# Start-up and last store of a fused attention and mixer kernel: first head's scores with decay by one-hot matmuls, a new order of the first pairs, moved fillers, last output in two parts

## The chip, the cores and the metric

The kernel runs on one core of one Trainium2 chip. The metric is the time of one execution on the device in microseconds.

## The reference

Attention with a causal mask and a learned decay (8 batches, 8 heads, 576 positions, head size 64), then a mixer: a low-rank mix along the sequence and a two-layer ReLU mix along the channels. Cut to what matters here:

```python
scores = (q @ k.T) / sqrt(D)
cum    = cumsum(maximum(s, 0))              # s: (batch, head, position)
scores = where(causal, -1e9, scores + minimum(-(cum[i] - cum[j]), 0))
x      = softmax(scores) @ v                # (B, S, H*D)
u      = x + (x.T @ U @ V).T                # low rank, along the sequence
out    = u + relu(u @ w_ch1) @ w_ch2        # 512 -> 2048 -> 512
```

The decay adds `cum[j] - cum[i]` to every score. The kernel folds it into the score matmul: beside the 64 rows of q and k it appends four rows, so that the contraction over 68 rows gives the product and the decay together.

## The kernel before

Heads come in pairs (`n`), 32 in all, four to a batch. The start handles the four pairs of batch 0 by hand; afterwards a loop weaves attention and mixer so that TensorE stays full. Only the start and the end are touched by the change. `...` marks cuts.

The rows of the decay for all 64 heads are made at once, one head to a partition, with the cumulative sum split in three bf16 parts so that no precision is lost. The first four pairs get them by DMA from SBUF to the `slot` tiles, where the score matmul reads them below the 64 rows of q and k:

```python
nc.vector.tensor_tensor_scan(cum, s_sb, s_sb, 0.0, op0=ALU.add, op1=ALU.max)
nc.scalar.mul(rows[:, 3, 0, :], cum, -1.0)
nc.vector.tensor_copy(rows[:, 0, 1, :], cum)          # three parts: rows 0, 1, 2
...
for n in range(PB):
    for hh in range(2):
        nc.sync.dma_start(out=slots[n][D:KA, hh, 0 : 2 * S], in_=rows[2 * n + hh : ...])
```

Scores of a pair are four groups, each followed by one exp on ScalarE: the near scores of either head (1,024 columns each), a wide group for both heads (1,024 columns) and a small one (128 columns). `pscore` tiles rotate through two buffers, `pwork` tiles through four.

```python
def scores(n, pT):
    for hh in range(2):
        near = pscore()
        ...                                            # six matmuls, slot[0:68]
        nc.scalar.activation(pT[:, hh, 0:1024], near, EXP, scale=scale)
        yield
    mid, tail = pscore(), pwork()
    ...                                                # wide group, exp; small group, exp
```

`spin` issues matmuls on constant data whose results nobody reads. The text calls them fillers. The start of batch 0, in program order, where `T` transposes a pair, `S` makes its scores, and `v_tiles` brings the raw values into the layout that the last attention matmul wants:

```python
spin_some(9); step(T0); spin_some(2); step(T0, T0); spin_some(8)
step(T1); spin_some(4); step(T1, T1); spin_some(2); step(T2, T2, T2); spin_some(2)
step(S0); spin_some(1, pwork); step(S0); spin_some(1, pwork); step(S0, S0)
masks(pT_of(0), False)                                 # on VectorE
spin_some(2, pwork); step(S1); spin_some(2, pwork); step(T3, T3, T3); step(S1)
spin_some(2, pwork); step(S1, S1); spin_some(2, pwork)
masks(pT_of(1), True); load_w1(1)                      # masks on GpSimd
step(S2, S2); spin_some(2, pwork); v_tiles(0, (0, 1), ...); step(S2, S2)
...
v_tiles(0, (2, 3), ...); step(S3); v_tiles(0, (4,), ...); step(S3)
drain(values(0, pT_of(0))); step(S3, S3)
```

The end writes 128 rows of 512 columns at a time: 16 matmuls, an add on VectorE, a store of 256 KB.

The softmax here doesn't subtract the row's maximum and nothing guards it: scores larger than these inputs give would overflow.

## Time and profile before

| | before |
|---|---|
| time, median of 3 (lowest to highest) | 385.93 us (385.05 to 386.65) |
| span of the profiled execution | 383.5 us |
| TensorE busy | 373.1 us, 97% |
| second layer and first layer of the channel mix | 138.9 + 134.9 us |
| first exp of scores | 12.85 us |
| last wide exp of the first batch | 25.71 us |

The page of the kernel before: busy time of each engine, then, in 40 equal slices of the span, the busy tenths of TensorE and the clock that was granted to it, then the two costliest groups (busy us and mean ns of one, then idle time just before them).

```profile
PE 373.1 (97%) x3562; PEld 210.2 (55%) x3562; DVE 224.6 (59%) x464; ACT 193.7 (51%) x291; POOL 64.7 (17%) x100
...
PE   8899999999999999999999999999999999999996
...
PEclk9999999999999999999999999999999999999999
...
L595 PE MATMUL pwork<-w_sb,hT 128*128 128x512 bf16 x576 | 138.9, 379 | 0.4 <-DVE slot L311 0.3
L585 PE MATMUL pwork<-uT,w_sb 128*128 128x512 bf16 x560 | 134.9, 379 | 0.6 <-DVE x_sb L400 0.3
```

TensorE shows 90% or more everywhere but in the first two slices and the last. The two large groups are 71% of the span and have almost no idle time before them, so nothing but the start and the end can give time without fewer matmuls.

The chain of waits of the kernel before, around the first exp (start us, us, what):

```profile
7.45 0.76 ACT slot L311
8.21 3.93 DMA slot<-hT
12.15 0.05 issue
12.19 0.63 PE pscore L334 x6
12.82 0.02 issue
12.85 1.03 ACT pT L348
```

The first scores wait 3.93 us for four rows of 2.3 KB. In that time ScalarE makes two copies (1.61 us, from 9.76) and is otherwise idle: 1.50 us before them and 1.48 us after them, until the first exp.

ScalarE's timeline of the kernel before, from there to the last exp of the batch (start us, us, what, count, and in brackets idle time before it with its releaser):

```profile
12.85 1.94 ACT L348 ACTIVATE pT<-pscore 128x1024 bf16<-128x1024 f32 x2 [1.48 <-PE pscore L334]
14.67 1.03 ACT L356 ACTIVATE pT<-pscore 128x1024 bf16<-128x1024 f32 x1
15.57 0.30 ACT L362 ACTIVATE pT<-pwork 128x128 bf16<-128x128 f32 x1
15.73 2.18 ACT L348 ACTIVATE pT<-pscore 128x1024 bf16<-128x1024 f32 x2
...
18.87 1.96 ACT L348 ACTIVATE hT<-pscore 128x1024 bf16<-128x1024 f32 x2
21.46 1.02 ACT L356 ACTIVATE hT<-pscore 128x1024 bf16<-128x1024 f32 x1 [0.63 <-PE pscore L334]
22.38 0.27 ACT L362 ACTIVATE hT<-pwork 128x128 bf16<-128x128 f32 x1
23.27 2.11 ACT L348 ACTIVATE hT<-pscore 128x1024 bf16<-128x1024 f32 x2 [0.61 <-PE pscore L334]
25.71 1.02 ACT L356 ACTIVATE hT<-pscore 128x1024 bf16<-128x1024 f32 x1 [0.34 <-PE pscore L334]
```

Read it as a relay. Up to 18.87 the exps follow each other, so ScalarE is the limit. From 21.46 on each begins after an idle time that TensorE ends: now TensorE's order is the limit, since it puts value selection and fillers between the score groups. The mixer cannot begin until the last exp here and the values after it are done.

The end, in the timeline of the kernel before:

```profile
376.35 0.69 DVE L632 TENSOR_TENSOR o_sb<-pwork,u_sd 128x512 f32<-128x512 f32 x1 [2.76 <-PE pwork L595]
377.07 3.79 SPq L649 DMA_DIRECT2D out_dram<-o_sb  x2
379.80 0.69 DVE L632 TENSOR_TENSOR o_sb<-pwork,u_sd 128x512 f32<-128x512 f32 x1 [2.76 <-PE pwork L595]
```

After the last matmul come the last add (0.69 us) and a store; its last landing in the trace is at 382.52, 2.72 us after that add began.

### The profile page before, as it was taken

The numbers are of one execution on the slowest core, as the hardware profiler recorded it, in microseconds if no ns is written. First come the engines' busy times: TensorE is split into PE (matmuls) and PEld (weight loads), VectorE is DVE, ScalarE is ACT, GpSimd is POOL, SyncE is SP. The second block draws the span as 40 slices with busy tenths as digits, with TensorE's granted clock in tenths as the row PEclk, the third lists the DMA queues.
The fourth block names the chain that finished last, engine by engine and source line by source line (L and its number), as shares of the span: only waits on it lengthen the run. The fifth ranks groups of instructions, "written<-read, shape, count | busy, mean of one in ns | idle before, by whom it ended". The sixth has DMA issues, their size and how long they took to land.

```text
span 383.5 us, 8466 instructions
## 1 busy us (share of the span) xinstructions
PE 373.1 (97%) x3562; PEld 210.2 (55%) x3562; DVE 224.6 (59%) x464; ACT 193.7 (51%) x291; POOL 64.7 (17%) x100
## 2 busy tenths in 40 slices
PE   8899999999999999999999999999999999999996
PEld 3565455665665666555655665666555544444442
DVE  8873556978778776777668766786663132002011
ACT  3865985356743576237733674357552520621610
POOL 8976316005100600060006000000000000000000
PEclk9999999999999999999999999999999999999999
DMA  7999999927992995299249933320323031302002
GB/s 113 161 210 186 195 174 106 166 63 110 147 56 72 163 150 42 70 172 152 34 53 161 173 41 49 95 77 20 62 59 99 19 81 58 82 28 83 0 29 82
DMA packets 85966, 37.29 MB, mean 97 GB/s; under 512 B 66408, under 2 KB 80200, under 8 KB 85928
## 3 DMA queue, kind: packets, MB, share of 16 engines
q0 software_dynamic: 47216, 18.44, 48.8%
q1 hardware_dynamic: 38712, 18.31, 24.9%
q8 instruction: 28, 0.46, 0.5%
q14 instruction: 10, 0.08, 0.1%
HBM read 37.25 MB, written 9.70 MB: 122 GB/s over the span
## 4 chain that ended last, share of the span: by engine, by line
PE 85%; DVE 7%; ACT 4%; DMA 2%; issue 1%; DVEq 0%; ACTq 0%; POOLq 0%
PE pwork L595 30%; PE pwork L585 30%; PE pscore L334 10%; PE pwork L390 6%; PE pwork L294 3%; DVE slot L311 3%; ACT pT L348 1%; DVE x_sb L400 1%; ACT slot L311 1%; DMA slot<-hT 1%; DMA q_sd<-in_q_dram 1%; PE pscore L585 1%; DVE uT L444 1%; PE pwork L516 1%; PE pwork L419 1%
## 5 line engine op out<-in xcount | busy, mean ns | idle before, releaser
L595 PE MATMUL pwork<-w_sb,hT 128*128 128x512 bf16 x576 | 138.9, 379 | 0.4 <-DVE slot L311 0.3
L585 PE MATMUL pwork<-uT,w_sb 128*128 128x512 bf16 x560 | 134.9, 379 | 0.6 <-DVE x_sb L400 0.3
L617 ACT ACTIVATE hT<-pwork 128x512 bf16<-128x512 f32 x140 | 84.4, 608 | 83.9 <-PE pwork L585 83.6
L311 DVE COPY slot<-pwork 64x576 bf16<-64x576 bf16 x118 | 94.4, 800 | 11.5 <-PE pwork L294 9.7
L348 ACT ACTIVATE pT<-pscore 128x1024 bf16<-128x1024 f32 x58 | 58.4, 1025 | 67.1 <-PE pscore L334 66.9
L595 PEld LDWEIGHTS <-hT 128*128 128x128 bf16 x576 | 50.6, 98 | 52.0 <-issue 2.2
L585 PEld LDWEIGHTS <-w_sb 128*128 128x128 bf16 x576 | 51.0, 98 | 51.0 <-issue 1.2
L632 DVE TENSOR_TENSOR o_sb<-pwork,u_sd 128x512 f32<-128x512 f32 x32 | 22.1, 690 | 67.5 <-PE pwork L595 66.5
L334 PE MATMUL pscore<-slot 68*128 68x128 bf16 (+4 forms) x512 | 55.9, 245 | 2.1 <-ACT slot L311 0.8
L334 PEld LDWEIGHTS <-slot 68*128 68x128 bf16 x576 | 42.4, 97 | 26.1 <-issue 2.3
L321 DVE TENSOR_TENSOR pT<-pT,keep 128x512 bf16<-128x512 bf16 (+1 forms) x84 | 29.5, 353 | 37.5 <-ACT pT L362 23.3
L390 PEld LDWEIGHTS <-pT 128*128 128x128 bf16 x870 | 32.4, 98 | 10.0 <-issue 0.3
L390 PE MATMUL pwork<-v_slot,pT 128*128 128x65 bf16 x870 | 34.6, 193 | 0.0
L356 ACT ACTIVATE pT<-pscore 128x1024 bf16<-128x1024 f32 x29 | 30.1, 1039 | 4.7 <-PE pscore L334 3.2
L400 DVE TENSOR_TENSOR x_sb<-pwork,rec 128x320 bf16<-128x320 f32 x64 | 31.3, 491 | 2.1
L108 POOL DMA_DIRECT2D q_sd<-in_q_dram x12 | 9.4, 782 | 126.8 <-PE pwork L294 117.1
L226 POOL DMA_DIRECT2D v_slot<-in_v_dram x24 | 21.4, 906 | 9.4 <-DMA w_sb<-in_moe_w_ch_dram 8.8
L294 PEld LDWEIGHTS <-q_sd 72*128 72x128 bf16 x256 | 15.1, 99 | 11.2 <-DMA q_sd<-in_q_dram 1.0
L399 DVE RECIPROCAL rec<-pwork 128x5 f32<-128x5 f32 x64 | 12.0, 190 | 15.4 <-PE pwork L390 14.8
L294 PE MATMUL pwork<-identity,q_sd 72*128 72x72 bf16 x256 | 18.2, 197 | 0.2
L294 PE MATMUL pwork<-identity,k_sd 72*128 72x72 bf16 x256 | 17.9, 197 | 0.3 <-DMA k_sd<-in_k_dram 0.3
L294 PEld LDWEIGHTS <-k_sd 72*128 72x128 bf16 x256 | 12.3, 98 | 0.9 <-DMA k_sd<-in_k_dram 0.4
(101 smaller groups left out, 191.8 us busy)
## 6 DMA issues: line engine op xcount, KB each, us to landing
out_dram<-o_sb SPq DMA_DIRECT2D x36, 256.0 KB
w_sb<-in_moe_w_ch_dram POOLq DMA_DIRECT2D x4, 1024.0 KB, 12.2
q_sd<-in_q_dram POOLq DMA_DIRECT2D x6, 576.0 KB, 8.9
k_sd<-in_k_dram POOLq DMA_DIRECT2D x6, 576.0 KB, 14.6
v_slot<-in_v_dram POOLq DMA_DIRECT2D x24, 128.0 KB, 15.8
hT<-in_v_dram POOLq DMA_DIRECT2D x2, 512.0 KB, 12.4
q_sd<-in_q_dram POOLq DMA_DIRECT2D x4, 144.0 KB, 4.5
k_sd<-in_k_dram POOLq DMA_DIRECT2D x4, 144.0 KB, 5.1
```

What stands on the lines that cost most here:

```text
L294: nc.tensor.transpose(tps[hh][:, c, t2, :], src[:, 2 * hp + hh, ds(t2 * 128, 128)], identity[:TP, :TP],)
L311: copies(n, hh, par)(dst[:, :, :, :, par], tp[par * D : par * D + D].rearrange("p c t m -> p c m t"),)
L321: nc.vector.tensor_tensor(dst, dst, keep[:, :, 0:w].to_broadcast([128, n_tiles, w]), op=ALU.min)
L334: nc.tensor.matmul(dst, lhsT=slot[0:KA, hh, ds(S + j * 128, 128)], rhs=slot[0:KA, hh, lo:hi], start=True, stop=True,)
L348: nc.scalar.activation(pT[:, hh, 0:1024], near, EXP, scale=scale)
L356: nc.scalar.activation(pT[:, :, 1024:1536], mid.rearrange("p (a b) -> p a b", a=2), EXP, scale=scale)
L390: nc.tensor.matmul(po[:, i, :], lhsT=pT[:, hh, ds(place(j, i), 128)], rhs=vt[:, j, h, :], start=(j == 0), stop=(j == i), skip_group_check= ...
L400: nc.vector.tensor_tensor(x_sb[:, hp, :, ds(hh * D, D)], po[:, :, 0:D], rec.to_broadcast([128, 5, D]), op=ALU.mult,)
L585: nc.tensor.matmul(f1, lhsT=w1_sb[:, kt, ds(nf * 128, 128)], rhs=u[:, kt, :], start=(kt == 0), stop=(kt == 3),)
L595: nc.tensor.matmul(f2, lhsT=hT[:, nf, ds(i * 128, 128)], rhs=w2_sb[:, nf, :], start=(nf == 0), stop=(nf == NF - 1 and not more), skip_grou ...
L617: nc.scalar.activation(hT[:, nf, :], f1, RELU)
L632: nc.vector.tensor_tensor(o_sb.rearrange("p (a b) -> p a b", a=4), f2.rearrange("p (a b) -> p a b", a=4), u_sd[:, :, i, :], op=ALU.add,)
```

## The change

Its intent: let the first head's exp run without waiting for the row DMA; put real work where fillers stood and fillers only where TensorE waits; shorten what follows the last matmul. The core of the diff:

```diff
+    def near_by_rows(hh, pT):
+        slot = slots[0]
+        one = identity[:BH, hh : hh + 1]               # picks head hh out of 64 partitions
+        near = pscore()
+        ...
+        for at, lo, hi in ((0, 0, 512), (512, 128, S), (960, 512, S)):
+            mm(at, hi - lo, one.to_broadcast([BH, 128]), rows[:, 3, 0, lo:hi], start=(at != 960))
+        for r in range(3):
+            ...
+            for j, at, lo, hi in blocks:
+                mm(at, hi - lo, rows[:, r, 1, ds(j * 128, 128)], one.to_broadcast([BH, hi - lo]))
+        ...                                            # then q and k, 64 rows, and the exp
```
```diff
-        on_act = hh == 0 and n in (0, 1, PB, PB + 1, PB + 3)
+        on_act = hh == 0 and (n in (0, 1, PB, PB + 1, PB + 3) or n == 2 and par == 0)
...                                                      # turn(), in transposes()
+                if (n, hh) == (3, 0):
+                    spin(2, tile)
...                                                      # scores(): first head of pair 0 left out;
+            if spins:                                   # pair 1 gets spins=(2, 3)
+                tail = tail or pwork()
+                spin(spins[hh], tail)
...                                                      # last output tile, in chanmix()
+                for lo, hi in ((0, 3), (3, 4)):         # 384 columns, then 128
+                    ...                                 # 16 matmuls, add, store
...                                                      # the start
+    spin_some(9); step(T0); spin_some(2); step(T0, T0)
+    step(A, A, A, A)                                    # A = near_by_rows(0, ...)
+    step(T1, T1, T1); step(T2); spin_some(5); step(T2, T2)
+    step(S0, S0, S0); step(T3, T3, T3); step(S1)
+    masks(pT_of(0), True); load_qk(1, 0, 4)             # masks on GpSimd, loads behind them
+    ...
+    step(S1); step(S1, S1); masks(pT_of(1), True); ...; load_w1(1)
+    v_tiles(0, (0, 1), ...); step(S2); step(S2); v_tiles(0, (2, 3), ...); step(S2, S2)
+    ...
+    v_tiles(0, (4,), ...); step(S3); step(S3); drain(values(0, pT_of(0))); step(S3, S3)
```

More of the change, by code (lines that the diff above doesn't have):

```diff
@@ L180 @@
         nc.vector.memset(slot[:KA, :, 2 * S :], 0.0)
-    nc.gpsimd.memset(slots[PB][D:KA, :, 0 : 2 * S], 1.0)
     v_slots = [consts.tile([128, 5, H, D + 1], BF16, name=f"v_slot{i}") for i in range(3)]
@@ L257 @@
     alloc_qk(1)
-    load_qk(1, 0, 4)
     init_v(nc.gpsimd, v_slots[0])
-    for pT in (*pTs, pT_early[0]):
-        nc.gpsimd.memset(pT[:, :, 1600:], 1.0)
     uT_of, x_of, xT_of = {}, {}, {}
@@ L288, in turn @@
             if c == 0:
-                tps[hh] = pwork().bitcast(BF16)[:, : 2 * 4 * TP].rearrange(
+                tile = pwork()
+                if (n, hh) == (3, 0):
+                    spin(2, tile)
+                tps[hh] = tile.bitcast(BF16)[:, : 2 * 4 * TP].rearrange(
                     "p (c t m) -> p c t m", c=2, t=4
@@ L328, in masks, with mm, scores @@
         mask(pT[:, :, 1536:1600], 2, 64, on_pool)
-    def scores(n, pT):
+    def near_by_rows(hh, pT):
+        slot = slots[0]
+        one = identity[:BH, hh : hh + 1]
+        near = pscore()
+        blocks = [(j, j * 128, j * 128, j * 128 + 128) for j in range(4)]
+        blocks += [(0, 512, 128, S), (3, 960, 512, S)]
+        def mm(at, w, lhsT, rhs, start=False, stop=False):
+            nc.tensor.matmul(
+                near[:, ds(at, w)],
+                lhsT=lhsT,
+                rhs=rhs,
+                start=start,
+                stop=stop,
+                skip_group_check=True,
+            )
+        for at, lo, hi in ((0, 0, 512), (512, 128, S), (960, 512, S)):
+            mm(
+                at,
+                hi - lo,
+                one.to_broadcast([BH, 128]),
+                rows[:, 3, 0, lo:hi],
+                start=(at != 960),
+            )
+        for r in range(3):
+            if r:
+                yield
+            for j, at, lo, hi in blocks:
+                mm(at, hi - lo, rows[:, r, 1, ds(j * 128, 128)], one.to_broadcast([BH, hi - lo]))
+        yield
+        for j, at, lo, hi in blocks:
+            mm(
+                at,
+                hi - lo,
+                slot[0:D, hh, ds(S + j * 128, 128)],
+                slot[0:D, hh, lo:hi],
+                stop=True,
+            )
+        nc.scalar.activation(pT[:, hh, 0:1024], near, EXP, scale=scale)
+        yield
+    def scores(n, pT, spins=()):
         slot = slots[n % NSLOT]
@@ L340, in mm @@
             )
-        for hh in range(2):
+        tail = None
+        for hh in range(2) if n > 0 else (1,):
             near = pscore()
@@ L350, in scores @@
                 mask(pT[:, hh, 0:512].rearrange("p (a b) -> p a b", a=4), 4, 128)
+            if spins:
+                tail = tail or pwork()
+                spin(spins[hh], tail)
             yield
-        mid, tail = pscore(), pwork()
+        mid, tail = pscore(), tail or pwork()
         for hh in range(2):
@@ L626, in chanmix @@
         for i in range(4):
+            if g == NG - 1 and i == 3:
+                o_sb = work.tile([128, DM], FP32, tag="o_sb", name="o_sb", bufs=3)
+                for lo, hi in ((0, 3), (3, 4)):
+                    f2 = pwork()
+                    for nf in range(NF):
+                        nc.tensor.matmul(
+                            f2[:, lo * 128 : hi * 128],
+                            lhsT=hT[:, nf, ds(i * 128, 128)],
+                            rhs=w2_sb[:, nf, lo * 128 : hi * 128],
+                            start=(nf == 0),
+                            stop=(nf == NF - 1),
+                        )
+                    nc.vector.tensor_tensor(
+                        o_sb[:, lo * 128 : hi * 128].rearrange("p (a b) -> p a b", b=128),
+                        f2[:, lo * 128 : hi * 128].rearrange("p (a b) -> p a b", b=128),
+                        u_sd[:, lo:hi, i, :],
+                        op=ALU.add,
+                    )
+                    nc.sync.dma_start(
+                        out=out_flat[ds(g * 512 + i * 128, 128), lo * 128 : hi * 128],
+                        in_=o_sb[:, lo * 128 : hi * 128],
+                    )
+                return
             f2 = ahead[i] if i in ahead else pwork()
@@ L694 @@
     act, dve = nc.scalar.copy, nc.vector.tensor_copy
-    S0, S1, S2, S3 = (scores(n, pT_of(n)) for n in range(PB))
+    S0, S1, S2, S3 = (scores(n, pT_of(n), (2, 3) if n == 1 else ()) for n in range(PB))
     T0, T1, T2, T3 = (transposes(n) for n in range(PB))
     M0, M1, M2, M3 = (mix_first(dt, act) for dt in range(PB))
+    A = near_by_rows(0, pT_of(0))
     spin_some(9)
@@ L701 @@
     step(T0, T0)
-    spin_some(8)
-    step(T1)
-    spin_some(4)
-    step(T1, T1)
-    spin_some(2)
-    step(T2, T2, T2)
-    spin_some(2)
-    step(S0)
-    spin_some(1, pwork)
-    step(S0)
-    spin_some(1, pwork)
-    step(S0, S0)
-    masks(pT_of(0), False)
-    spin_some(2, pwork)
-    step(S1)
-    spin_some(2, pwork)
+    step(A, A, A, A)
+    step(T1, T1, T1)
+    step(T2)
+    spin_some(5)
+    step(T2, T2)
+    step(S0, S0, S0)
     step(T3, T3, T3)
     step(S1)
-    spin_some(2, pwork)
+    masks(pT_of(0), True)
+    load_qk(1, 0, 4)
+    for pT in (*pTs, pT_early[0]):
+        nc.gpsimd.memset(pT[:, :, 1600:], 1.0)
+    step(S1)
     step(S1, S1)
-    spin_some(2, pwork)
     masks(pT_of(1), True)
+    nc.gpsimd.memset(slots[PB][D:KA, :, 0 : 2 * S].bitcast(mybir.dt.uint32), 0x3F803F80)
     load_w1(1)
-    step(S2, S2)
-    spin_some(2, pwork)
     v_tiles(0, (0, 1), (dve, dve))
+    step(S2)
+    step(S2)
+    v_tiles(0, (2, 3), (dve, dve))
     step(S2, S2)
@@ L730 @@
     nc.gpsimd.memset(pT_early[1][:, :, 1600:], 1.0)
-    v_tiles(0, (2, 3), (dve, dve))
+    v_tiles(0, (4,), (dve,))
     step(S3)
-    v_tiles(0, (4,), (dve,))
     step(S3)
@@ L737 @@
     masks(pT_of(3), True)
+    drain(values(1, pT_of(1)))
     load_w2(0)
@@ L740 @@
     load_qk(1, 4, 4)
-    drain(values(1, pT_of(1)))
     step(M0)
```

## The prediction

> **What bounds it now.** The page: TensorE 97% busy at full granted clock; the two output-mixer groups alone take 274 of 383.5 us. That bulk is untouched: from the fourth pair's last scores to the last output tile the instruction order stays, apart from one memset and one row DMA. Only the start (0 to 26 us) and the last 4 us can give time.
>
> Start, by the chain of waits and the timeline: slot copy to 8.21, rows to slot 0 by DMA until 12.15, first exp 12.85. Then four pairs' exps on ScalarE, the last wide one 25.71. Without gaps a pair takes 2.9 us (starts 0.91 apart, 0.16 for the small one), so from 15.73 the floor is 24.4; PE's order adds the rest (fillers 0.22 us each, value selection 1.0 us per two tiles). A VectorE chain follows to 30.6.
>
> **What the change does.**
> 1. The first head's exp no longer waits for the row DMA. 27 matmuls, 5 x 1024 columns, cost about 2.2 us of PE (a 1024-column score group took 0.44). Rows are ready at 6.1, 7.3, 8.1, the slot copy at 8.26: exp at 9.25, where ScalarE idled. 0.92 us leave the exp chain behind the DMA; 0.35 is lost, as the second head's row lands at 12.50.
> 2. A copy of 0.80 us moves to ScalarE; the VectorE copy behind it waits to about 12.6, so slots 2 and 3 are ready near 15.0 and 18.2 (14.8, 19.6 before).
> 3. Pair 0's masks go to GpSimd (0.63 us per wide one), next-batch loads behind them. DMA is backlogged from 12 to 77 us, so landings hardly move: first w1 half 24.4, needed 31.1; second 33.0, needed 41.1; next q/k 47.0, needed 50.3. Slacks exceed the shift.
> 4. Seven fillers remain of twelve after the first score; value selection moves ahead of pair 2's scores.
>
> By these durations: second head's exp 13.2, pair 1 from 15.2 (15.73), then PE limits: pair 2 from 19.0 (18.87), pair 3 from 21.9 (23.27), its wide last exp 24.1 (25.71). Gain 1.65 us, carried to the end: later work is unchanged.
>
> 5. Tail now: last matmul 379.78, add 0.69, store packets 381.4 to 382.2, landed 382.5, end 383.5. After: 384 columns, then 128; PE columns equal, last add about 0.25, 64 KB instead of 256 KB last. Gain 0.7 us (0.45 add, 0.25 packets), an estimate. [...]
>
> **Prediction.** 385.9 - 1.65 - 0.7 = 383.6 us, 382.4 to 385.2 (8 in 10). Faster by over 2%: 0.01; within: 0.985; slower: 0.005.
>
> **What would show it.** First exp at 9 to 9.5; second head's at 13.2; last wide exp of pair 3 near 24.1; first mixer matmul near 29.4 instead of 31.1; same shift at 100 and 300 us; last add 0.2 to 0.3 us.
>
> **What would make it wrong.** [...] I expect 1.2 us idle before 12.5; here fillers take 0.43 us until 5.8, 0.22 afterwards. Also: broadcast one-hots slower than plain matmuls; a GpSimd mask or a buffer later than estimated; the gain absorbed around 45 to 90 us, where ScalarE and VectorE limit; run scatter of 0.8 us.

The sum is whole: 385.9 - 1.65 - 0.7 = 383.55, put as 383.6. The 1.2 us idle was the reason for not fearing that the clock would fall.

## The result

| | before | after |
|---|---|---|
| time, median | 385.53 us (4 runs) | 383.07 us (4 runs, 382.81 to 383.22) |
| span of the profiled execution | 383.5 us | 381.3 us |
| last wide exp of the first batch | 25.71 | 24.07 |
| start of last add to last landing | 2.72 us | 1.90 us |

The ratio is 0.9931, 95% interval 0.9907 to 0.9956: faster by 0.7%, the same within 2%. A ratio here is always the mean time of one kernel's runs over that of the other's of the same rounds, so it is not quite the ratio of the medians quoted. Executions over 1.5% slower than the fastest of the same kernel are left out of the means.

The page of the changed kernel, the same lines:

```profile
PE 371.3 (97%) x3583; PEld 210.8 (55%) x3583; DVE 223.6 (59%) x461; ACT 194.6 (51%) x292; POOL 65.1 (17%) x103
...
PE   8899999999999999999999999999999999999997
...
PEclk9999999999999999999999999999999999999999
...
L640 PE MATMUL pwork<-w_sb,hT 128*128 128x512 bf16 x560 | 135.4, 379 | 0.4 <-DVE slot L310 0.3
L630 PE MATMUL pwork<-uT,w_sb 128*128 128x512 bf16 x560 | 134.9, 379 | 0.6 <-DVE x_sb L445 0.3
```

The bulk is as it was; 16 of the second layer's 576 matmuls have become 32 narrower ones and stand in another group.

The chain of waits of the changed kernel, at the same place:

```profile
9.09 3.37 DMA slot<-hT
12.46 0.05 issue
12.50 0.63 PE pscore L375 x6
13.13 0.02 issue
13.15 1.02 ACT pT L390
```

The row DMA is still on the chain, but it is now the second head's.

ScalarE's timeline of the changed kernel:

```profile
9.34 1.02 ACT L368 ACTIVATE pT<-pscore 128x1024 bf16<-128x1024 f32 x1 [1.24 <-PE pscore L337]
10.26 2.42 ACT L310 COPY slot<-pwork 64x576 bf16<-64x576 bf16 x3
13.15 1.02 ACT L390 ACTIVATE pT<-pscore 128x1024 bf16<-128x1024 f32 x1 [0.47 <-PE pscore L375]
14.07 1.02 ACT L401 ACTIVATE pT<-pscore 128x1024 bf16<-128x1024 f32 x1
14.98 0.28 ACT L407 ACTIVATE pT<-pwork 128x128 bf16<-128x128 f32 x1
15.14 1.04 ACT L390 ACTIVATE pT<-pscore 128x1024 bf16<-128x1024 f32 x1
16.39 1.02 ACT L390 ACTIVATE pT<-pscore 128x1024 bf16<-128x1024 f32 x1 [0.21 <-PE pscore L375]
...
19.05 1.94 ACT L390 ACTIVATE hT<-pscore 128x1024 bf16<-128x1024 f32 x2 [0.38 <-PE pscore L375]
21.00 1.02 ACT L401 ACTIVATE hT<-pscore 128x1024 bf16<-128x1024 f32 x1
21.92 0.27 ACT L407 ACTIVATE hT<-pwork 128x128 bf16<-128x128 f32 x1
22.14 1.94 ACT L390 ACTIVATE hT<-pscore 128x1024 bf16<-128x1024 f32 x2
24.07 1.02 ACT L401 ACTIVATE hT<-pscore 128x1024 bf16<-128x1024 f32 x1
```

The first exp has moved into ScalarE's idle time. From 13.15 to the last wide exp it now takes 10.92 us (24.07 - 13.15) instead of 12.86 (25.71 - 12.85). The idle times of 0.63, 0.61 and 0.34 us are gone.

The end, in the timeline of the changed kernel:

```profile
377.57 0.56 DVE L684 TENSOR_TENSOR o_sb<-pwork,u_sd 128x384 f32<-128x384 f32 x1 [1.91 <-PE pwork L677]
378.16 0.96 SPq L690 DMA_DIRECT2D out_dram<-o_sb  x2
378.47 0.29 DVE L684 TENSOR_TENSOR o_sb<-pwork,u_sd 128x128 f32<-128x128 f32 x1 [0.34 <-PE pwork L677]
```

The last add is 0.29 us; the last landing is at 380.37, 1.61 us after that add ends.

How the gain travels, by the starts of the same ScalarE instructions in the two traces: 1.64 us at the last wide exp, 1.41 at 35 us, 1.38 at 100 and at 200, 1.37 at 366. So 0.23 us go between 29.4 and 30.1, and nothing after that. In the profile, TensorE stops there for 0.24 us between two first-layer matmuls without waiting for anything that the profile shows.

### The profile page after: what moved, and what is told of

Its sections match the earlier page's. It is cut to its first block, busy times and chain, and to the rows that moved or that the text cites. A ratio compares the mean times of both kernels' runs of the same rounds, so it can differ in the third digit from the quotient of the medians.

```text
span 381.3 us, 8511 instructions
## 1 busy us (share of the span) xinstructions
PE 371.3 (97%) x3583; PEld 210.8 (55%) x3583; DVE 223.6 (59%) x461; ACT 194.6 (51%) x292; POOL 65.1 (17%) x103
## 4 chain that ended last, share of the span: by engine, by line
PE 85%; DVE 8%; ACT 3%; DMA 2%; issue 1%; SPq 0%; DVEq 0%; ACTq 0%
PE pwork L630 30%; PE pwork L640 29%; PE pscore L375 10%; PE pwork L435 6%; DVE slot L310 3%; PE pwork L293 3%; DVE x_sb L445 1%; ACT pT L390 1%; PE pscore L630 1%; PE pwork L677 1%; DMA slot<-hT 1%; DVE uT L489 1%; ACT slot L310 1%; DMA hT<-in_s_dram 1%; PE pwork L561 1%
## 5 line engine op out<-in xcount | busy, mean ns | idle before, releaser
L640 PE MATMUL pwork<-w_sb,hT 128*128 128x512 bf16 x560 | 135.4, 379 | 0.4 <-DVE slot L310 0.3
L390 ACT ACTIVATE pT<-pscore 128x1024 bf16<-128x1024 f32 x57 | 57.5, 1025 | 65.9 <-PE pscore L375 65.9
L640 PEld LDWEIGHTS <-hT 128*128 128x128 bf16 x560 | 49.0, 98 | 50.1 <-issue 2.2
L375 PE MATMUL pscore<-slot 68*128 68x128 bf16 (+1 forms) x506 | 54.9, 246 | 1.8 <-ACT slot L310 0.8
L320 DVE TENSOR_TENSOR pT<-pT,keep 128x512 bf16<-128x512 bf16 (+1 forms) x81 | 28.6, 354 | 37.0 <-ACT pT L407 22.8
L401 ACT ACTIVATE pT<-pscore 128x1024 bf16<-128x1024 f32 x29 | 30.1, 1037 | 5.0 <-PE pscore L375 3.5
## 6 DMA issues: line engine op xcount, KB each, us to landing
w_sb<-in_moe_w_ch_dram POOLq DMA_DIRECT2D x4, 1024.0 KB, 13.2
```

Of the source, the lines that this page charges most:

```text
L320: nc.vector.tensor_tensor(dst, dst, keep[:, :, 0:w].to_broadcast([128, n_tiles, w]), op=ALU.min)
L375: nc.tensor.matmul(dst, lhsT=slot[0:KA, hh, ds(S + j * 128, 128)], rhs=slot[0:KA, hh, lo:hi], start=True, stop=True,)
L401: nc.scalar.activation(pT[:, :, 1024:1536], mid.rearrange("p (a b) -> p a b", a=2), EXP, scale=scale)
L640: nc.tensor.matmul(f2, lhsT=hT[:, nf, ds(i * 128, 128)], rhs=w2_sb[:, nf, :], start=(nf == 0), stop=(nf == NF - 1 and not more), skip_grou ...
```

## The experiments

Twelve kernels ran in three groups, each group on one chip and timed in five rounds against the kernel before (medians of before 385.39, 385.48 and 385.23). All gave correct results. One number serves throughout, called the stretch: the time from the start of the first exp that needs a row DMA to the start of pair 3's last wide exp. It leaves out when the rows land, which differs between executions by some tenths of a microsecond (the first row-fed exp starts between 12.53, in a0, and 13.41, in e3; later only in e12, at 14.40). It is no constant either: two profiles of the changed kernel differ in it by 0.49 us (10.92, and 11.41 in a0), so a smaller difference between single profiles is weak evidence unless the trace shows its cause.

| run | time, median | ratio to before, 95% | first row-fed exp | last wide exp | stretch |
|---|---|---|---|---|---|
| kernel before | 385.53 | | 12.85 | 25.71 | 12.86 |
| changed kernel | 383.07 | 0.9931 (0.9907 to 0.9956) | 13.15 | 24.07 | 10.92 |
| e1, tail only | 384.49 | 0.9976 (0.9954 to 0.9998) | 12.91 | 25.77 | 12.86 |
| e2, start only | 383.66 | 0.9961 (0.9936 to 0.9986) | 12.81 | 23.73 | 10.92 |
| e8, one-hot matmuls only | 384.74 | 0.9989 (0.9963 to 1.0016) | 13.10 | 25.11 | 12.01 |
| e3, all but one-hot matmuls | 383.56 | 0.9945 (0.9922 to 0.9969) | 13.41 | 25.13 | 11.72 |
| a0, changed kernel again | 382.91 | 0.9935 (0.9909 to 0.9962) | 12.53 | 23.94 | 11.41 |
| e5, copy back on VectorE | 382.56 | 0.9919 (0.9894 to 0.9944) | 13.13 | 24.05 | 10.92 |
| e6, masks back on VectorE | 382.71 | 0.9925 (0.9882 to 0.9967) | 12.70 | 23.77 | 11.07 |
| e10, fillers in own tile | 383.13 | 0.9930 (0.9889 to 0.9972) | 12.98 | 23.94 | 10.96 |
| e12, tail in halves | 383.38 | 0.9937 (0.9896 to 0.9977) | 14.40 | 25.32 | 10.92 |
| e4, no fillers in pair 1 | 386.13 | 0.999 (0.9943 to 1.0037) | 12.77 | 27.62 | 14.85 |
| e7, no fillers after the first eleven | 388.54 | 1.0082 (1.0058 to 1.0107) | 12.75 | 29.29 | 16.54 |
| e9, no fillers before pair 1 | 390.44 | 1.0112 (1.0066 to 1.0157) | 13.18 | 31.69 | 18.51 |

In before, e1 and e3 the stretch holds one exp more (both heads of pair 0), 0.92 us.

### Which part gives what: e1, e2, e8, e3

My theory: tail and start add up; in the start the one-hot matmuls and the new order each give a part. Rivals: the one-hot matmuls are all of it, or only TensorE's order counts.

**e1_tail_only**, the kernel before with the last output in two parts:

```diff
         for i in range(4):
+            if g == NG - 1 and i == 3:
+                ...                                    # 384 columns, then 128
```

> The kernel before with the last output in two parts, nothing else. My theory (tail and start gains are separate and add): last add 0.29 us instead of 0.69, last store lands 0.4 us sooner after it; time 0.85 us under before (about 384.7), the last wide exp of pair 3 unmoved at 25.7. Rival (the tail is free only because the whole run is shifted, or its gain is noise): under 0.3 us.

Measured: 384.49, ratio 0.9976. Stretch and last wide exp are those of before; last add 0.29 us, and from its start to the last landing 1.90 us instead of 2.72. The tail's gain is real and independent of the start.

**e2_start_only**, the changed kernel without that block:

```diff
-            if g == NG - 1 and i == 3:
-                ...
```

> The changed kernel with its last output in one part again. My theory: last wide exp of pair 3 at 24.1, gain 1.4 to 1.65 us under before (about 384.0), the shift constant from 40 us to the end; with the tail-only run it adds up to the whole change's 2.4. In the profile of the changed kernel 0.24 us of the shift is lost at 29.4 to 30.1 on a TensorE stop that names no wait; if that is chance, it need not be here and the shift stays 1.65; if it belongs to the order, it is here too. Rival (start gain absorbed later): under 0.7 us.

Measured: 383.66, ratio 0.9961. Start of last add to last landing is 2.72 us again. The stretch is 10.92. The last wide exp is 1.98 us earlier than before, as the rows happened to land earlier in this execution, and 1.96 us are left at 366 us: what the start gives is carried to the end. The stop of 0.24 us at the first layer is not here.

**e8_rows_only**, the kernel before with the first head's near scores by one-hot matmuls in place of eight fillers:

```diff
     step(T0, T0)
-    spin_some(8)
+    step(A, A, A, A)
...
-        for hh in range(2):
+        for hh in range(2) if n > 0 else (1,):
```

> The kernel before with only the first head's near scores by one-hot matmuls (they replace eight fillers), its order, masks, loads and tail otherwise kept. My theory: first exp near 9.3, second head 13.2, pair 1 from 15.2, wide exp of pair 2 about 20.7 instead of 21.5, last wide exp of pair 3 about 25.0 instead of 25.7; gain 0.7 us, 384.8. Rival 1 (rows are all of the start gain): 1.6 us, 383.9. Rival 2: none, 385.5.

Measured: 384.74, and the last wide exp at 25.11. The time alone cannot tell this from before (the interval holds 1), the profile can: the stretch is 0.85 us shorter (12.86 - 12.01), for the exp that has left it. It begins later, since it needs the second head's rows, which landed 0.35 us after the first's in the trace of before. About half a microsecond remains.

**e3_no_rows**, the changed kernel with the first head's scores from the slot rows as before, eight fillers in place of the one-hot matmuls:

```diff
-    step(A, A, A, A)
+    spin_some(8)
...
-    step(S0, S0, S0)
+    step(S0, S0, S0, S0)
```

> The changed kernel, but the first head's near scores come from the slot rows by DMA as before, with eight fillers in place of the one-hot matmuls. My theory by the same arithmetic as the prediction: first exp 12.85, pair 1 from 15.7, pair 2 from 19.5, last wide exp of pair 3 at 24.6; 0.55 us slower than the changed kernel (about 383.6). Rival 1 (the one-hot matmuls are the whole start gain): 1.6 us slower, 384.7. Rival 2 (only the new order of PE counts): no slower, 383.1.

Measured: 383.56. One of the six executions is slow (391.47 us, granted clock 0.978); it is left out of the ratio, though not of the median. First exp 13.41 and last wide exp 25.13, both later than expected because the rows landed later in this execution; the stretch is 11.72, where the expectation had 11.75 (24.6 - 12.85). The order alone shortens it by 1.14 us (12.86 - 11.72).

So both rivals fall, by the profiles; the times alone do not separate them. The two parts add up: 0.85 + 1.14 = 1.99, against 1.94 for the whole (12.86 - 10.92), which is closer than the scatter of the stretch gives a right to expect. In the changed kernel's profile the later row-fed exp (13.15 against 12.85) takes 0.30 of it back.

### Parts that were thought to matter: e5, e6

**e5_copy_on_dve**:

```diff
-        on_act = hh == 0 and (n in (0, 1, PB, PB + 1, PB + 3) or n == 2 and par == 0)
+        on_act = hh == 0 and n in (0, 1, PB, PB + 1, PB + 3)
```

> The changed kernel with slot 2's first copy back on VectorE. My theory: VectorE then does four copies of slot 2 from about 11.9 instead of three from 12.7, both end near 15.1, ScalarE is idle anyway before 13.1: no change, within 0.15 us in the profile's 10.9 us stretch. Rival (the moved copy makes pair 2 ready sooner): 0.5 to 0.8 us slower.

Measured: stretch 10.92, time 382.56 (a0 in the same rounds: 382.91). Moving that copy gives nothing. In the changed kernel VectorE's next copy waits for it until 12.71.

**e6_masks_dve**:

```diff
-    masks(pT_of(0), True)
+    masks(pT_of(0), False)
```

> The changed kernel with pair 0's masks on VectorE again, at the same place in the order. My theory: they take about 1 us there after slot 3's copies, so the copies of the selected values start near 19.5 instead of 18.5, but the tiles and values are still ready when PE asks (20.8 and about 22.7): no change, the stretch from the second head's exp to pair 3's last wide exp stays 10.9 within 0.15 us. Rival (moving the masks to GpSimd is a needed part of the gain): 0.5 to 1 us longer and slower.

Measured: stretch 11.07, time 382.71. Inside the 0.15 us allowed, at its edge. The trace shows a small cost: at 20.78 TensorE waits 0.21 us for a copy of VectorE, which it does not do in the changed kernel. The rival's 0.5 us does not show, but this is one profile, and the interval of the times is wider than that. The mask move is at most a small part.

**a0_after**, the changed kernel as control:

> The changed kernel as it is, for control beside the other three on one chip. Time 2.3 us under before. Every theory: from the second head's exp to the start of pair 3's last wide exp 10.9 us, as in the two profiles that have this order. The stop of TensorE of 0.24 us near 29.4 that names no wait was in one of five profiles; if it is chance it is not here.

Measured: 382.91. The stretch missed the expectation: 11.41 instead of 10.92. The rows were early here (first row-fed exp 12.53), but pair 2 began at 18.92, as in the other profiles (18.59 to 19.05). The instruction ahead of pair 2's scores is the selection of raw values, whose first load landed at 17.16 here and at 16.28 to 16.96 in the other six profiles of this order; TensorE idles 0.45 us before it here, which is nearly the whole miss, and does not wait for it in the others. So when rows come early and the values late, the value load is the next limit; this is read from the order and the landing, and no run moved that load. The stop near 30.1 is here again, of 0.37 us, and the gain falls by as much (1.77 us at the last wide exp, 1.41 at 50 us). So it is not mere chance of one execution: it is in two of the seven profiles that have this order and ran past 30 us in it. In those two the trace's fetch of instructions (queue q8) begins at 27.6 to 27.8, in four of the others at 25.9 to 26.3 (the fifth, e12, began later as a whole). What stops TensorE is not shown.

### Are the fillers needed: e4, e7, e9

The change's intent is to put fillers only where TensorE waits. By my arithmetic pair 1's five fillers stood in TensorE's way. The rivals of e4 and e7 were that without the fillers the granted clock falls.

**e4_no_s1_fillers**:

```diff
-    S0, S1, S2, S3 = (scores(n, pT_of(n), (2, 3) if n == 1 else ()) for n in range(PB))
+    S0, S1, S2, S3 = (scores(n, pT_of(n)) for n in range(PB))
```

> The changed kernel without the five fillers between the scores of pair 1. My theory (PE's order is the limit there and the fillers stand in it; the clock needs none of them): pair 2's first exp about 5.2 us after the second head's exp instead of 5.9, last wide exp of pair 3 after about 10.2 instead of 10.9, fillers and matmuls still 0.22 us apart; 0.7 us faster than the changed kernel (about 382.4). Rival [...]: 512-column matmuls at 0.43 us for some us after 16, 1 us or more slower. Second rival (they only fill waits, as the change's text says): no change, within 0.2 us.

Measured: six executions at 386.72, 387.93, 385.70, 386.57, 382.42 and 382.30, with granted clocks of 0.987, 0.987, 0.991, 0.987, 1.0 and 1.0. My theory held for the two at full clock and fell for four; the first rival is right for these. Stretches of four microseconds in the profile of the first (length; busy us and number of instructions of TensorE, its weight loads, VectorE, ScalarE and GpSimd; then the granted clock, the DMA share, which this view lets exceed 1, and GB/s):

```profile
14.00:18.00 4.00, 3.18 (x36) 2.00 (x33) 3.90 (x6) 3.79 (x6) 3.90 (x10) 1.00 1.49 208
18.00:22.00 4.00, 4.00 (x25) 1.80 (x23) 2.50 (x5) 1.94 (x2) 3.88 (x9) 0.52 1.10 211
22.00:26.00 4.00, 4.00 (x39) 2.63 (x37) 1.29 (x3) 2.93 (x4) 2.10 (x5) 0.50 1.20 197
26.00:30.00 4.00, 4.00 (x85) 3.75 (x83) 2.69 (x9) 1.40 (x3) 1.76 (x3) 0.70 1.09 205
```

And the same of the control, the changed kernel:

```profile
14.00:18.00 4.00, 3.38 (x34) 2.01 (x31) 3.90 (x6) 3.80 (x6) 3.90 (x11) 1.00 1.46 211
18.00:22.00 4.00, 4.00 (x40) 2.07 (x36) 3.42 (x6) 3.09 (x5) 3.88 (x9) 1.00 1.13 216
22.00:26.00 4.00, 3.97 (x105) 3.67 (x105) 2.96 (x11) 3.13 (x5) 3.31 (x8) 1.00 1.20 199
```

Without five fillers (about 1.1 us, five of 0.22) the granted clock halves at 18.2 us and stays so for 10.24 us. "Busy" shows nothing of it: 4.00 of 4.00 us either way, with 25 matmuls in one and 40 in the other.

**e7_no_fillers_at_all**, also without the seven before pair 1:

```diff
-                if (n, hh) == (3, 0):
-                    spin(2, tile)
...
-    spin_some(5)
```

> The changed kernel without the five fillers of pair 1, the two before pair 3's transposes and the five before pair 2's second transposes; only the first eleven stay. My theory: as the run without pair 1's fillers, within 0.15 us, since the other seven stand where PE waits for rows or buffers; clock stays full, matmuls 0.22 us apart. Rival [...]: 0.43 us per 512-column matmul afterwards and 1 to 3 us slower than the changed kernel.

Measured: 388.54, all six between 388.41 and 389.70. My theory fell, and the rival is right with a larger size than it gave: half clock from 13.2 us for 17.07 us. The longest gap between two matmul starts shortly before was 1.18 us.

**e9_no_early_fillers**, without those seven but with pair 1's five:

> The changed kernel without the seven fillers before pair 1 (five, two), with pair 1's five kept. Theory formed after the last four runs [...]: the clock halves near 12 to 14 us as in the run without any, for 10 us or more, and the time is 4 to 6 us over the changed kernel (387 to 389) in most executions. Rival (only pair 1's fillers matter): no change, 382.9.

Measured: 390.44, all six between 389.58 and 390.93, half clock from 11.0 us for 20.48 us. The theory held (the clock halves, at 11.0 us instead of 12 to 14), with a larger loss than its 387 to 389. That is worse than without any fillers: at half clock a filler costs twice as much (0.43 us) and did not bring the clock back. Part of the difference from e7 is only that more executions have the longer loss (granted clock 0.973 or 0.974 in four of six, in e7 in two of six); at equal granted clock (0.978) e9 took 389.6 and e7 about 388.5, on different chips.

Neither TensorE's idle time nor its longest gap tells which way the clock goes. In four microseconds before or around the drop TensorE was idle for 0.82 us in e4 (14 to 18, drop at 18.2), 1.30 in e7 (10 to 14, drop at 13.2) and 1.24 in e9 (8 to 12, drop at 11.0); the changed kernel kept the full clock with 0.93 (11.5 to 15.5). And e3 kept it across 1.99 us between two matmul starts (waiting for q, until 11.06), where e7 lost it with 1.18. So the runs show that taking out fillers brought the clock to half in the profiles of e4, e7 and e9, and its mean down to 0.973 to 0.991 in four of six executions of e4 and all six of e7 and of e9; what in TensorE's work decides it, they do not show.

### A better version, and the tail: e10, e12

**e10_fillers_in_own_tile**, e5's edit, and pair 1's fillers write the tile of the scores that follow:

```diff
             near = pscore()
+            if spins and hh == 1:
+                spin(spins[0], near[:, 0:512])
...
-        mid, tail = pscore(), tail or pwork()
+        mid, tail = pscore(), pwork()
+        if spins:
+            spin(spins[1], mid[:, 0:512])
```

> A try at a better version: slot 2's first copy back on VectorE, and pair 1's five fillers write the tile of the scores that follow, so they no longer wait for pair 0's small exp. Theory: the second exp of pair 1 0.1 to 0.25 us earlier, the stretch to pair 3's last wide exp 10.6 to 10.9, bounded by the landing of the raw values near 17.0 to 17.3; clock stays full; time within 0.4 us of the changed kernel, lower if at all. Rival [...]: clock halves after 18 us in some executions, 386.

Measured: 383.13, stretch 10.96, full clock. The gap before pair 1's second exp is gone, but 0.28 us stand before its wide one, and pair 2 begins at 18.91 as ever. No gain. The value load is not what bounds it, against my expectation: it landed at 16.29 and 16.64, and TensorE began the selection at 17.29 straight after pair 1's last scores. TensorE's own order does: the last three fillers now begin at 16.05, after pair 1's first exp has released their buffer (15.98).

**e12_tail_halves**:

```diff
-                for lo, hi in ((0, 3), (3, 4)):
+                for lo, hi in ((0, 2), (2, 4)):
```

> The changed kernel with the last output in halves of 256 columns instead of 384 and 128. Theory (the end is last add, then one store's fixed time, then its packets): last add 0.42 us (0.29 for 128 columns, 0.56 for 384), from the start of the last add to the last landing about 2.05 to 2.15 us instead of 1.90, 0.15 to 0.25 us worse at the end than the changed kernel: within the noise of the times, seen in the profile. Rival (any split does as well): 1.9.

Measured: last add 0.42 us and 2.16 us from its start to the last landing, against 1.90 with 384 and 128 and 2.72 with one part. The times cannot tell it (383.38); the profile agrees with the theory, a hair above its range, and the rival's 1.9 does not show. From the end of the last add to the last landing the traces give 1.61 us for 64 KB (changed kernel), 1.74 for 128 KB (e12) and 2.03 for 256 KB (before).

This profile brought something nobody expected. The kernel's start is the changed kernel's, yet in this execution (384.27 us) the clock halved:

```profile
7.00:11.00 4.00, 3.14 (x49) 2.18 (x47) 3.70 (x6) 2.72 (x5) 3.92 (x7) 0.97 1.07 156
11.00:14.00 3.00, 2.82 (x17) 1.64 (x17) 0.47 (x1) 1.40 (x2) 3.00 (x6) 0.50 0.85 112
14.00:18.00 4.00, 3.64 (x42) 2.42 (x42) 3.72 (x5) 3.56 (x6) 3.52 (x9) 0.98 1.46 204
```

For about 3.4 us, from 10.75, TensorE ran at half clock, and the first row-fed exp came at 14.40 instead of about 13. The third pair's q landed at 10.44 (9.56 to 10.17 in the other six profiles of this order), so the five fillers behind it began at 11.18, after the clock had halved. So the changed kernel can lose the clock too; that the late load of q brought it on is my reading of one trace, and not shown. The record shows how often the clock is lost, as it has the granted clock of every execution, where this loss makes 0.996. It is 0.996 or lower in 7 of 40 executions of the kernels with this start (changed kernel, a0, e2, e5, e6, e10, e12), which are all but one of those above 384 us, and in 7 of 33 of the kernel before in these rounds. So the kernel before loses the clock as well; where in the kernel an unprofiled execution lost it is not on record.

## Why the prediction was right

The time lay within 0.6 us of the prediction, in its range, and the profile bears out most steps, not only the sum. That the sum is so close is in part luck: in the profiles the start is worth 1.37 us at the end (1.65 forecast) and the tail 0.82 (0.7), errors of opposite sign.

1. *First exp at 9.25, in ScalarE's idle time.* Measured 9.34. The one-hot matmuls run at the speed of plain ones: 1,024 columns of them took 0.44 us (6.52 to 6.96), as a plain near group did (0.44). e8 gives this part as 0.85 us of the stretch; the prediction had 0.92, and 0.35 lost to the second head's rows.
2. *Copy moved to ScalarE.* The wait of VectorE came as stated (12.71), and e5 shows that the move gives nothing.
3. *Masks and loads on GpSimd; landings hardly move.* First half of w1 landed at 24.43 (24.37 before), second at 33.89 (32.96), next q and k at 46.62 (46.97). In the trace of before the DMA share, which can exceed 1, is 1.16 to 2.45 in stretches from 12 to 77 us and 0.12 from 77 to 85. The slacks held, and the shift of 1.38 us at 100 us is nearly the 1.41 of 35 us. e6 shows that the masks could have stayed for about 0.15 us.
4. *By these durations: pair 1 from 15.2, pair 2 from 19.0, pair 3 from 21.9, last wide exp 24.1.* Measured 15.14, 19.05, 22.14, 24.07. e3 and e8 show both terms of this sum by themselves. The count of fillers holds only after the first row-fed score: seven, of twelve; counted from the very first score there are twelve in both kernels.
5. *Tail 0.7 us (0.45 add, 0.25 packets).* Measured 0.82 in the profile (2.72 to 1.90): 0.40 for the add and 0.42 for the store, so the packets' term was too small. The sentence cut there was about the rest of the store; the traces give that only as a whole, 1.61 us for 64 KB after the add.
6. *Carried to the end.* Nearly: of 1.64 us 1.37 are left at the end of the changed kernel's profile, the rest lost at one stop of TensorE. e2, without the stop, keeps 1.96 of 1.98.

What the prediction had wrong did not show in its number. It named a lower clock as a risk of fewer fillers and dismissed it with "1.2 us idle". e7 lost the clock with no gap over 1.18 us, and e4 with none over 0.68, while e3 kept it across 1.99. With the fillers that the change keeps, the granted clock was above 0.996 in 33 of 40 executions; without the seven, without the five or without both it was 0.973 to 0.991 in 16 of 18. My later theory, that pair 1's fillers were dead weight, fell in e4, where four executions of six lost the clock. The changed kernel is faster since the first head's exp no longer stands behind the row DMA, TensorE's order no longer delays ScalarE between 21 and 26 us, and the last add and store are smaller; the change took out 16 fillers of 39 and kept enough. Transposing the third pair sooner was not run by itself; it is within the 1.14 us of e3.

## What to carry to other kernels

When the first matmul of a chain waits for a small DMA that only moves rows to other partitions, a one-hot matmul on the data where it lies can do the same sooner, if TensorE has time: here the exp came at 9.34 instead of 12.85, and e8 shortened the stretch by 0.85 us. Before deleting matmuls that compute nothing, look at the granted clock, not at busy time: in a stretch where TensorE waits often their worth may appear only when they are gone, here as half clock for 10.24 to 20.48 us: without five fillers of 0.22 us each, four executions of six took 2.8 to 5.0 us longer than the control (e4). Judge such a start by more than one execution, since the other two of e4 kept the full clock, and read each execution's granted clock. Split the last store unevenly, with the small part last: 1.90 us from the last add to the last landing here, against 2.16 with halves (e12).
